# Two attention and dense layers on one core: unread matmuls by the share of the array in use, and a finer table for the banks that VectorE exponentiates

## The chip, the cores and the metric

The kernel runs on one core of a Trainium2 chip. A core has TensorE (PE, matmuls, with PEld for its weight loads), VectorE (DVE), ScalarE (ACT), GpSimd (POOL) and SyncE (SP, which issues the DMAs). The metric is the device time in microseconds of one execution; the time of a version is the median of several executions. The profile shows one execution, with every instruction's start and duration and the clock that was granted to TensorE.

## The reference

The input x has 2048 rows of 448 numbers. Four steps follow one another, each added to x: attention, dense, attention, dense, with the same weights both times.

```python
def _A_ref(x, wqkv, wo):              # H = 16 heads of Dh = 28
    qkv = (x @ wqkv) ...              # q, k, v
    scores = einsum("bhqd,bhkd->bhqk", q, k) * Dh ** -0.5
    p = softmax(scores, axis=-1)
    o = einsum("bhqk,bhkd->bhqd", p, v)
    return o @ wo                     # heads side by side
def _B_ref(x, w1, b1, w2, b2):        # 448 -> 1792 -> 448
    h = x @ w1 + b1
    r = where(h > 0, h, 0)
    return (r * r) @ w2 + b2
x = x + _A_ref(_layernorm(x), A_wqkv, A_wo)
x = x + _B_ref(_layernorm(x), B_w1, B_b1, B_w2, B_b2)
...                                   # both once more
```

The scores are 2 x 16 x 2048 x 2048 numbers, and each of them goes through an exponential.

## The kernel before, in words

**Units and groups.** Scores are made transposed, keys on partitions. A unit is 128 partitions by 512 scores of one head (two key blocks by 256 queries, or four by 128 for the two narrow query blocks at the end), one PSUM bank. There are 2048 units, in passes: a pass is a layer, a query block, four heads that lie on the four row strips of TensorE, and a range of key blocks. `s_stream` takes the units three at a time; such a group has 683 instances. Its score matmuls (L916) use 32 of the 128 rows each, and three strips run side by side. `e_stream` lets ACT take the exponential of a whole group in one instruction (L941). `p_stream` multiplies the probabilities with V (L1080), 128 rows by 32 columns, four heads side by side, and evicts the sums.

**Banks for VectorE.** ACT need not do all. In a group, the function `apart` may give the third bank to VectorE, which computes an exponential in three operations (`a_unit`, `a_rest`): L995 shifts and clamps, L1008 squares the fraction, L1016 adds and writes the bits of a bf16 number. `apart` says no when, among other things, VectorE's backlog (its clock ahead of now, plus what is left of earlier exponentials) exceeds `PACE` at the present place: `PACE` is a table that is spread evenly over the 2048 units. Then ACT takes the third bank as well. The buffers in which VectorE works and the places for its result are limited too (`sets_of`, `pd_free`).

**Everything else** runs in the gaps: layer norm (VectorE, a little POOL), transposes (L551), projections and the dense step in tiles of `mm_tile` (L647) with evictions on VectorE, the spread of the softmax denominators by DMAs, and the sums over w1 (`sums`, L379: 56 matmuls with a single moving column, in seven operations), which are needed for the last block.

**The order of the work** is written by a planner that runs on the host when the kernel is built. Each stream offers its next operation (`Op`) with an engine, a planned duration, what it depends on and which buffer it takes. The planner places the candidate that can start earliest, ties by priority, and holds back TensorE work that would make the next scores late. The order that comes out is fixed in the program; on the chip only semaphores decide when each instruction starts.

**Unread matmuls.** The clock granted to TensorE is not always full (in one stretch of this profile it is 0.50), and the kernel holds matmuls whose result nobody reads, placed by how much TensorE has lately done in the plan. There are two kinds. In `s_stream` a group's score matmuls are repeated, up to `MORE` = 3 times, when `load(HWIN)`, the share of the last 3.4 us in which TensorE was occupied in the plan, is under `HOT` = 0.9 (`HOTE` = 0.8 for the last 100 units), and only as often as they fit before the next TensorE operation and before the buffer's end. In `heat`, the stream of the lowest priority, one or two 448-column matmuls (L1501) are offered after a group when `load(WINDOW)`, over 2.8 us, is under `HEAT` = 0.76. They take one of the two spare PSUM banks for as long as they run.

Of the kernel before, what the change touches and what calls it, by code (L numbers as in the profile page):

```python
# [23 lines left out]


FRAC = 7
EXP_MID = 0.506
EXP_LOW = 128.0 * 128
EXP_SHIFT = 184.0 * 128 - round(EXP_MID * 2.0 ** 16) / 512
# [11 lines left out]
OWN = 2  # L41
HALF = 320
TURNS = 1
ENDU = 100
HOTE = 0.8
WSTOP = ('rs', 0)
XT = 0
VEND = 1
# [3 lines left out]
EARLY = 3  # L52
AHEAD = (range(0, 4), range(0, 4), range(0, 4), range(0, 1))
SLACK = 0.5
WINDOW = 2.8
C_PRIO = 1.6
V_PRIO = 8.5
V_LATE = 5.2
# [13 lines left out]
LEAD = 15  # L72
LAST = 690
BUSY = 0.995
PACE = (3.6, 3.6, 3.6, 1.8, 1.8, 1.8, 1.8, 1.8, 0.3, 0.9, 2.2, 2.2, 2.2, 2.6, 3.0, 3.0, 3.0, 3.6, 6.0, 2.2, 2.2, 2.2, 4.5, 2.2, 3.0, 2.6, 2.2, 2.2, 2.6, 2.6, 1.8, 1.8, 2.2, 2.6, 2.6, 1.8, 1.8, 1.8, 2.2, 2.6, 3.0, 6.0, 2.6, 4.5, 1.4, 1.4, 1.4, 1.4, 1.4, 1.4, 1.4, 1.4, 2.2, 2.2, 2.2, 2.2, 2.2, 2.2, 2.2, 2.2, 2.2, 2.2, 2.2, 2.2)
SPAN = 11
NPT = 11
NOS = 2
AEND = 0
HOT = 0.9  # L80
MORE = 3
HEAT = 0.76
HWIN = 3.4
NEAR_U = 0
LASTP = 3.2
HOLD = 5
# [34 lines left out]


class Op:
    __slots__ = ("eng", "dur", "fn", "deps", "acq", "rel", "mode", "sets", "start", "end", "res", "turn", "ready", "lat", "need", "got", "more", "room")

    def __init__(self, eng, dur, fn, deps=(), acq=None, rel=None, mode="full", sets=(), lat=0.0, need=1):
        self.eng = eng if isinstance(eng, tuple) else (eng,)
        self.dur, self.fn, self.deps, self.mode, self.lat = dur, fn, deps, mode, lat
        self.rel = rel if isinstance(rel, list) else ([] if rel is None else [rel])
        self.acq = acq if isinstance(acq, tuple) or callable(acq) else (() if acq is None else (acq,))  # L130
        self.sets = sets if isinstance(sets, list) else ([sets] if sets else [])
        self.start = self.end = self.res = self.turn = None
        self.need, self.got, self.more = need, [], 0.0


LAT = {"PE": 0.25, "ACT": 0.22, "DVE": 0.10, "POOL": 0.15, "DMA": 2.0, "-": 0.0}
# [2 lines left out]
class Planner:  # L139
# [3 lines left out]
    def __init__(self):  # L143
        self.clock = {"PE": 0.0, "ACT": 0.0, "DVE": 0.0, "POOL": 0.0, "DMA": 0.0, "-": 0.0}
        self.mode = None
        self.tok = {}
        self.streams = []
        self.past = {"PE": [], "DVE": []}
        self.turns = lambda: False
        self.slack = lambda: SLACK  # L150

    def load(self, span, eng="PE"):

        now = self.clock["PE"]
        return sum(min(e, now) - max(s, now - span) for s, e in self.past[eng] if e > now - span and s < now) / span

    def spawn(self, prio, gen):
        self.streams.append([prio, gen, next(gen, None)])
        self.streams.sort(key=lambda s: s[0](0.0) if callable(s[0]) else s[0])

    def earliest(self, o):
        t = 0.0
        for d in o.deps:
            if not isinstance(d, Op):
                d = self.tok.get(d)
            if d is None or d.end is None:
                return None, None
            same = d.eng[0] == o.eng[0] and len(o.eng) == 1
            t = max(t, d.end + d.lat + ((0.03 if same else 0.10) if d.eng[0] == "DVE" else
                                (0.0 if same and d.eng[0] != "DMA" else LAT[d.eng[0]])))  # L170
        acq = o.acq() if callable(o.acq) else o.acq
        if o.acq:
            free = [r.when() for r in acq if r.when() is not None]
            if not free:
                return None, None
            t = max(t, min(free))
        o.ready = t
        best = None
        for e in o.eng:
            s = max(t, self.clock[e])  # L180
            if e == "PE" and self.mode != o.mode:
                s = max(t, self.clock[e] + 0.1)
            if best is None or s < best[0] - 0.05:
                best = (s, e)
        return best

    def run(self):
        while self.streams:
            cands = []
            for st in self.streams:  # L190
                s, e = self.earliest(st[2]) if st[2] is not None else (None, None)
                if s is not None:
                    cands.append((s, st[0](s) if callable(st[0]) else st[0], e, st))
            assert cands, "no stream can go on"
            known = cands

            due = next((c[3][2].ready for c in cands if c[1] == 0), None)
            if due is None:
                due = next((c[0] + c[3][2].dur + LAT["ACT"] for c in cands if c[1] == 1), None)
            if due is not None:  # L200
                ok = [c for c in cands if c[2] != "PE" or c[1] == 0 or c[0] + c[3][2].dur <= due + self.slack()]
                cands = ok or cands
            s, _, e, st = min(cands, key=lambda c: (max(c[3][2].ready, self.clock[c[2]]) if c[2] == "PE" and self.turns() else c[0], c[1]))
            o = st[2]
            o.eng = (e,)
            if o.acq:
                o.res = min((r for r in (o.acq() if callable(o.acq) else o.acq) if r.when() is not None), key=lambda r: r.when())
                o.turn = len(o.res.rel)
                o.res.rel.append(None)
            o.start, o.end = s, s + o.dur  # L210
            if e == "PE":
                o.room = min([c[0] for c in known if c[2] == "PE" and c[3] is not st] or [1e9]) - o.end
            if o.fn:
                o.fn(e)
            o.end += o.more
            self.clock[e] = o.end - (OVER if e == "DVE" and o.dur > 0.1 else 0.0)
            if e == "PE":
                self.mode = o.mode
            if e in self.past:
                self.past[e] = [p for p in self.past[e] if p[1] > s - 40.0] + [(s, max(s, self.clock[e]))]  # L220
            for a in o.rel:
                a.got.append(o.end + o.lat + LAT[e])
                if len(a.got) == a.need:
                    a.res.rel[a.turn] = max(a.got)
            for key in o.sets:
                self.tok[key] = o
            st[2] = next(st[1], None)
            if st[2] is None:
                self.streams.remove(st)
# [3 lines left out]
def kernel(  # L233
# [43 lines left out]
    pl = Planner()  # L277
# [503 lines left out]
    units = []  # L781
# [69 lines left out]
    def s_stream():  # L851
        while at[0] < len(units):
# [5 lines left out]
            def fn(e, gi=gi, us=us, js=js):  # L858
# [41 lines left out]
                    if len(where[pi, kb]) == G:  # L900
                        pl.tok["u", pi, kb] = o

                short = (HOT if len(units) - at[0] > ENDU else HOTE) - pl.load(HWIN)
                again = 0
                if short > 0 and gi > 0:
                    last = ("e" in gbuf[gi - 1] and gbuf[gi - 1]["e"].end) or pl.clock["ACT"] + 1.35
                    again = max(0, min(MORE, int(min(o.room, last - LAT["PE"] - 0.05 - o.end) / 0.22)))
                o.more = 0.22 * again
                for i in list(range(4)) * (again + 1):
                    for k, (pi, kb, r, hh) in enumerate(us):  # L910
                        if i >= r:
                            continue
                        l, qb, g, *_ = passes[pi]
                        t0, nt = blocks[l][qb]
                        rows = slice(DHP * hh, DHP * hh + DHP)
                        nc.tensor.matmul(dst[k][:, i * nt * P:(i + 1) * nt * P],  # L916
                                         lhsT=K_sb[l][rows, g, (kb + i) * P:(kb + i + 1) * P],
                                         rhs=Q_sb[rows, g, t0 * P:(t0 + nt) * P],
                                         start=True, stop=True, tile_position=(DHP * hh, 0))
# [32 lines left out]
    def pd_free(unit):  # L952

        pi, kb, r, hh = unit
        l, qb, *_ = passes[pi]
        if l == 0:
            return (R_pd[0], *(R_pd[1:5] if qb <= 6 else R_pd[3:5]))
        if len(norm_done.get((0, len(blocks[0]) - 1), ())) < G:
            return tuple(R_pd[:1])
        return tuple(R_pd[:1] + R_pd[6:]) if hidden_left[0] else tuple(R_pd[:1] + R_pd[5:])  # L960
# [44 lines left out]
    def a_rest(gi, c, box, unit):  # L1005
# [10 lines left out]
            nc.vector.scalar_tensor_tensor(out=box["two"](pd.bitcast(DT.int16)), in0=box["i"], scalar=EXP_BITS, in1=box["h"],  # L1016
                                           op0=ALU.add, op1=ALU.add)
        own = gbuf[gi]["in"]
        o = Op("DVE", 0.683, close, deps=[h, ("e", gi)] if own else [h], acq=None if own else lambda: pd_free(unit), rel=c, sets=("x", gi))
        gbuf[gi]["x"] = o  # L1020
        yield o
        left[0] -= 0.6
# [6 lines left out]
    def p_stream():  # L1029


        for pi, (l, qb, g, kbs, first, last) in enumerate(passes):
# [19 lines left out]
            while todo:  # L1052
# [16 lines left out]
                def fn(e, now=now, begin=begin, close=close, box=box, pi=pi, l=l, g=g, r=r, n=n):  # L1069
# [4 lines left out]
                    for kb in now:  # L1074
# [13 lines left out]
                       deps=[*by, *{("V", l, kb + i) for kb in now for i in range(r)}],  # L1088
                       acq=None if "o" in box else pools_now(),
                       rel=[gbuf[gi]["e" if w == "x" and gbuf[gi]["in"] else w] for w, gi in by], mode="col")  # L1090
                box.setdefault("o", o)
                yield o
            if last and quick(l, qb, g):
# [392 lines left out]
    def heat():  # L1486


        for gi in itertools.count(HFROM):
            if not s_left:  # L1490
                return
            yield Op("-", 0.0, None, deps=[("s", gi)])
            short = HEAT - pl.load(WINDOW)
            if short <= 0 or not s_left or len(units) - at[0] < HSTOP:
                continue
            k = 1 if short < 0.14 else 2

            def junk(e):
                t = bank(o, "mt")
# [53 lines left out]
```

## Time and profile before

| | |
|---|---|
| median of three executions | 849.33 us (848.26 to 850.94) |
| the profiled execution | 848.74 us, its span 847.0 us |
| mean granted clock | 0.994 |
| ACT busy | 826.4 us, of it 815.7 us in 683 exponentials |
| VectorE busy | 793.7 us |
| exponentials of 3 banks / of 2 banks | 438 / 245 |
| score matmuls / products with V | 5180 / 4352 |
| unread 448-column matmuls (L1501) | 128 |

The span is the time from the first to the last instruction; the rest of the execution's time lies around it. TensorE's busy time counts each matmul with its modelled length, fill and drain included, so it is far from saying that the array streams all that time. In a window's row stand its bounds and length, each engine's busy time with the number of instructions, the granted clock, and the DMA engines' share. In a group's row stand the line of the kernel, the engine, the operation, what it writes and reads, the shape and count, then the busy time and the mean length of one in ns, and the idle time just before them with what ended it. In a waits row stand who waited for whom, the total, how many times, and the longest.

### The profile page before, as it was taken

What the parts mean: (1) busy time and instruction counts of PE and PEld (TensorE: products, weight loads), DVE (VectorE), ACT (ScalarE), POOL (GpSimd) and SP (SyncE); (2) the same over time, 40 slices, a digit from 0 to 9 for tenths busy, and PEclk for the clock granted to TensorE, in tenths of its full rate; (3) what the DMA queues carried; (4) which work ended last, traced back from release to release, by engine and by line L of the source; (5) the groups of instructions that cost most, each with busy time, mean ns of one, the idle gap of its engine ahead of it and who ended that gap; (6) DMA issues with size and microseconds to landing.
All of it is one profiled execution on the core that took longest, in us unless ns stands there. A gap on an engine that the chain in (4) does not pass through costs nothing.

```text
span 847.0 us, 27977 instructions
## 1 busy us (share of the span) xinstructions
PE 809.2 (96%) x12200; PEld 430.6 (51%) x12200; DVE 793.7 (94%) x1563; ACT 826.4 (98%) x699; POOL 41.7 (5%) x94
## 2 busy tenths in 40 slices
PE   8999999999999999999999999998999999999997
PEld 4455555554545545454445554444554454545565
DVE  7999999999999999999899999989999999999965
ACT  8998999999999999999999999999999999999994
POOL 3100000000000010000000000001000000000000
PEclk9999999999999999999999999989999999999999
DMA  9200000000000000000000000011000000000000
GB/s 250 67 2 3 19 24 16 15 16 15 11 6 15 15 16 15 16 3 14 2 3 2 2 2 2 15 30 28 18 24 25 21 21 21 21 13 15 21 9 19
DMA packets 32363, 17.97 MB, mean 21 GB/s; under 512 B 17833, under 2 KB 31787, under 8 KB 32240
## 3 DMA queue, kind: packets, MB, share of 16 engines
q1 hardware_dynamic: 32240, 16.18, 6.9%
q8 instruction: 95, 1.56, 0.8%
q14 instruction: 28, 0.23, 0.1%
HBM read 13.88 MB, written 2.07 MB: 19 GB/s over the span
## 4 chain that ended last, share of the span: by engine, by line
PE 48%; ACT 27%; DVE 15%; issue 7%; DMA 2%; POOL 1%; ACTq 0%; SPq 0%; DVEq 0%
ACT pt L941 27%; PE mt L647 20%; PE sc L916 16%; PE oT L1080 8%; DVE v_i L995 2%; DVE v_h L1008 2%; PE mt L1501 2%; DVE r L1274 1%; DVE pt L1016 1%; DVE K_sb L1008 1%; DVE K_sb L995 1%; DVE st L501 1%; DVE x_sb L1216 1%; DMA rec<-scr 1%; DVE xn L611 1%
## 5 line engine op out<-in xcount | busy, mean ns | idle before, releaser
L941 ACT ACTIVATE pt<-sc 128x1536 bf16<-128x1536 f32 (+1 forms) x683 | 815.7, 1415 | 6.8 <-PE sc L916 6.2
L916 PE MATMUL sc<-Q_sb,K_sb 32*128 32x256 bf16 (+1 forms) x5180 | 306.8, 267 | 27.6 <-ACT pt L941 21.5
L916 PEld LDWEIGHTS <-K_sb 32*128 32x128 bf16 x5180 | 131.6, 92 | 205.9 <-issue 153.1
L1080 PE MATMUL oT<-pt,V_sb 128*32 128x256 bf16 (+1 forms) x4034 | 154.5, 270 | 0.7 <-DVE pt L1016 0.3
L995 DVE TENSOR_SCALAR v_i<-sc 128x512 f32<-128x512 f32 x175 | 119.1, 682 | 6.9 <-PE sc L916 6.1
L647 PE MATMUL mt<-xnT,w 128*128 128x256 bf16 (+1 forms) x888 | 120.3, 271 | 1.0 <-DVE r L1274 0.5
L1008 DVE SCALAR_TENSOR_TENSOR v_h<-v_i 128x512 f32<-128x512 int16 x175 | 117.5, 679 | 0.5
L1080 PEld LDWEIGHTS <-V_sb 128*32 128x32 bf16 x4352 | 90.9, 96 | 50.0 <-issue 46.9
L647 PEld LDWEIGHTS <-w 128*128 128x128 bf16 x896 | 74.3, 98 | 37.7 <-issue 28.9
L1274 DVE TENSOR_SCALAR r<-mt 128x512 bf16<-128x512 f32 x108 | 73.4, 680 | 4.7 <-PE mt L647 4.4
L647 PE MATMUL mt<-w,V_sb 128*128 128x448 bf16 (+1 forms) x288 | 69.3, 348 | 0.0
L995 DVE TENSOR_SCALAR K_sb<-sc 128x512 f32<-128x512 f32 x69 | 47.1, 683 | 3.1 <-PE sc L916 2.4
L528 POOL TENSOR_TENSOR ve<-mv,eps_t 128x2 f32<-128x2 f32 (+1 forms) x33 | 11.5, 348 | 769.3 <-DVE mv L506 769.3
L1008 DVE SCALAR_TENSOR_TENSOR K_sb<-K_sb 128x512 f32<-128x512 int16 x69 | 46.8, 678 | 0.3
L1216 DVE TENSOR_TENSOR x_sb<-x_sb,mt 128x448 bf16<-128x448 bf16 x62 | 37.6, 611 | 7.3 <-PE mt L647 6.8
L1501 PE MATMUL mt<-xn,ident 128*128 128x448 bf16 x128 | 44.1, 357 | 0.3
L1016 DVE SCALAR_TENSOR_TENSOR pt<-v_i,v_h 128x512 int16<-128x512 f32 x64 | 43.0, 672 | 0.3
L1016 DVE SCALAR_TENSOR_TENSOR V_sb<-v_i,v_h 128x512 int16<-128x512 f32 x63 | 42.5, 678 | 0.2
L501 DVE BATCH_NORM_STATS2 st<-x_sb 128x6 f32<-128x448 bf16 x63 | 38.5, 614 | 0.8 <-DMA x_sb<-in_A_x_dram 0.7
L647 PEld LDWEIGHTS <-V_sb 128*128 128x128 bf16 x302 | 24.2, 98 | 25.0 <-issue 11.0
L647 PE MATMUL mt<-wo,oTn 128*128 128x448 bf16 x124 | 31.2, 355 | 0.4 <-DVE r L1274 0.3
L647 PEld LDWEIGHTS <-wk 128*128 128x128 bf16 x256 | 22.2, 97 | 11.4 <-issue 8.3
(133 smaller groups left out, 704.1 us busy)
## 6 DMA issues: line engine op xcount, KB each, us to landing
rec<-scr SPq DMA_DIRECT2D x54, 128.0 KB
x_sb<-in_A_x_dram SPq DMA_DIRECT2D x8, 224.0 KB
out_dram<-x_sb SPq DMA_DIRECT2D x15, 112.0 KB
w<-in_B_w_dram SPq DMA_DIRECT2D x1, 1568.0 KB
w<-in_B_w_dram SPq DMA_DIRECT2D x1, 1344.0 KB
dn<-oT_sb SPq DMA_DIRECT2D x54, 4.0 KB
V_sb<-in_A_wqkv_dram SPq DMA_DIRECT2D x4, 168.0 KB
scr<-dn SPq DMA_DIRECT2D x27, 8.0 KB
```

Source lines behind the costliest of these rows:

```text
L501: nc.vector.bn_stats(out=box["st"][:, :], in_=x_sb[:, t0 + j, :] if src is None else src())
L528: nc.gpsimd.tensor_tensor(out=ve[:, a:b], in0=mv[0][:, a:b, 1], in1=eps_t[:, a:b], op=ALU.add)
L647: nc.tensor.matmul(box["t"][:, c0:c0 + n], lhsT=lhsT() if callable(lhsT) else lhsT, rhs=rhs, start=a, stop=b)
L916: nc.tensor.matmul(dst[k][:, i * nt * P:(i + 1) * nt * P], lhsT=K_sb[l][rows, g, (kb + i) * P:(kb + i + 1) * P], rhs=Q_sb[rows, g, t0 * P: ...
L941: t = nc.scalar.activation(out=pt[:, 0:n], in_=gbuf[gi]["sc"][:, 0:n], func=AF.Exp, scale=float(np.log(2.0)) * 2.0 ** -FRAC)
L995: t = nc.vector.tensor_scalar(out=box["i"], in0=two(src), scalar1=EXP_SHIFT, scalar2=EXP_LOW, op0=ALU.add, op1=ALU.max)
L1008: nc.vector.scalar_tensor_tensor(out=box["h"], in0=box["f"], scalar=EXP_BEND, in1=box["f"], op0=ALU.mult, op1=ALU.mult)
L1016: nc.vector.scalar_tensor_tensor(out=box["two"](pd.bitcast(DT.int16)), in0=box["i"], scalar=EXP_BITS, in1=box["h"], op0=ALU.add, op1=ALU.add)
L1080: nc.tensor.matmul(box["t"][DHP * hh:DHP * hh + DHP, 0:n], lhsT=V_sb[l][:, kb + i, 4 * g + hh, :], rhs=p[:, c0:c0 + n], start=begin and kb ...
L1216: nc.vector.tensor_tensor(out=x_sb[:, tb, lo:hi], in0=x_sb[:, tb, lo:hi], in1=t[:, 0:hi - lo], op=ALU.add)
L1274: nc.vector.tensor_scalar(out=r[:, 0:w], in0=t[:, 0:w], scalar1=0.0, scalar2=None, op0=ALU.max)
L1501: nc.tensor.matmul(t[:, 0:D], lhsT=ident[:, :], rhs=xns[0][:, 0:D], start=True, stop=True)
```

## The change

TensorE's planned use is now measured by how much of its array works. The planner keeps a list `used` of the last TensorE operations with a weight: the time that the same work would take if it filled all of the array. `warm` sums these weights over the last `TICK` = 1.8 us. Scores have 0.0533 us per bank (and repeat), products with V 0.2133 us per step, and all other operations `SHARE` = 0.9 of their planned duration. Both kinds of unread matmuls are added when `warm` is under 0.55; `heat` adds two instead of one when the share is short by more than 0.055 (before 0.14). The constants of the old rule go.

The table `PACE` has 128 entries instead of 64. Their mean is 1.96 instead of 2.38; 75 of the 128 stretches have a lower entry than before, 30 a higher one, 23 the same.

The third operation of VectorE's exponential gets a latency of `XL` = 0.1 us in the plan, for what depends on it and for the buffers that it frees. The planner also keeps the time at which an operation's inputs are there (`base`) rather than working it out each time; that is a matter of the host alone. Since the plan is made step by step, each edit can move everything that is placed after it.

```diff
+XL = 0.1
+TICK = 1.8
+WARM = 0.55
+WARM2 = 0.55
+SHARE = 0.9
...
-ENDU = 100
-HOTE = 0.8
...
-WINDOW = 2.8
...
-PACE = (3.6, 3.6, 3.6, 1.8, 1.8, 1.8, 1.8, 1.8, 0.3, 0.9, 2.2, 2.2, 2.2, 2.6, 3.0, 3.0, 3.0, 3.6, 6.0, 2.2, 2.2, 2.2, 4.5, 2.2, 3.0, 2.6, 2.2, 2.2, 2.6, 2.6, 1.8, 1.8, 2.2, 2.6, 2.6, 1.8, 1.8, 1.8, 2.2, 2.6, 3.0, 6.0, 2.6, 4.5, 1.4, 1.4, 1.4, 1.4, 1.4, 1.4, 1.4, 1.4, 2.2, 2.2, 2.2, 2.2, 2.2, 2.2, 2.2, 2.2, 2.2, 2.2, 2.2, 2.2)
+PACE = (2.2, 2.2, 2.2, 2.2, 2.2, 2.2, 1.0, 1.8, 2.2, 1.0, 2.6, 1.4, 2.2, 1.4, 1.4, 2.2, 2.2, 2.6, 3.0, 1.8, 1.0, 2.6, 2.6, 1.4, 2.2, 2.2, 1.4, 1.4, 1.8, 1.8, 2.2, 1.4, 1.8, 1.4, 0.6, 1.4, 1.8, 1.4, 1.4, 2.2, 1.8, 1.8, 1.8, 3.0, 3.0, 2.2, 2.2, 2.2, 2.2, 2.2, 2.2, 2.2, 2.2, 1.8, 1.8, 2.2, 2.2, 2.2, 2.2, 1.4, 1.4, 2.2, 2.2, 3.0, 3.0, 2.2, 1.8, 1.8, 2.2, 2.2, 1.8, 1.0, 1.0, 1.4, 2.6, 1.8, 1.8, 2.2, 2.2, 1.8, 1.8, 1.8, 1.0, 2.2, 1.8, 3.0, 3.0, 1.8, 1.8, 0.6, 1.0, 1.8, 1.4, 1.4, 0.6, 3.0, 2.2, 1.8, 1.4, 1.4, 0.6, 3.0, 3.0, 1.8, 1.8, 1.8, 1.8, 2.6, 1.4, 1.4, 1.4, 2.2, 2.2, 1.8, 2.2, 1.8, 1.4, 1.8, 1.8, 3.6, 3.6, 3.0, 3.0, 1.4, 2.2, 2.2, 2.2, 2.2)
...
-HOT = 0.9
...
-HEAT = 0.76
-HWIN = 3.4
...
+    def warm(self):
+
+        now = self.clock["PE"]
+        return sum(w * (min(e, now) - max(s, now - TICK)) / (e - s) for s, e, w in self.used if e > now - TICK and s < now) / TICK
...
+            if e == "PE" and o.end > s:
+                self.used = [u for u in self.used if u[1] > s - 2 * TICK] + [(s, o.end, SHARE * o.dur if o.w is None else o.w)]
...
-                short = (HOT if len(units) - at[0] > ENDU else HOTE) - pl.load(HWIN)
+                short = WARM2 - pl.warm()
                 again = 0
                 if short > 0 and gi > 0:
                     last = ("e" in gbuf[gi - 1] and gbuf[gi - 1]["e"].end) or pl.clock["ACT"] + 1.35
                     again = max(0, min(MORE, int(min(o.room, last - LAT["PE"] - 0.05 - o.end) / 0.22)))
                 o.more = 0.22 * again
+                o.w = 0.0533 * len(us) * (again + 1)
...
-        o = Op("DVE", 0.683, close, deps=[h, ("e", gi)] if own else [h], acq=None if own else lambda: pd_free(unit), rel=c, sets=("x", gi))
+        o = Op("DVE", 0.683, close, deps=[h, ("e", gi)] if own else [h], acq=None if own else lambda: pd_free(unit), rel=c, sets=("x", gi), lat=XL)
...
+                o.w = 0.2133 * len(now)
...
-            short = HEAT - pl.load(WINDOW)
+            short = WARM - pl.warm()
             if short <= 0 or not s_left or len(units) - at[0] < HSTOP:
                 continue
-            k = 1 if short < 0.14 else 2
+            k = 1 if short < 0.055 else 2
```

More of the change, by code (lines that the diff above doesn't have):

```diff
@@ L123 @@
 class Op:
-    __slots__ = ("eng", "dur", "fn", "deps", "acq", "rel", "mode", "sets", "start", "end", "res", "turn", "ready", "lat", "need", "got", "more", "room")
+    __slots__ = ("eng", "dur", "fn", "deps", "acq", "rel", "mode", "sets", "start", "end", "res", "turn", "ready", "lat", "need", "got", "more", "room", "base", "w")
     def __init__(self, eng, dur, fn, deps=(), acq=None, rel=None, mode="full", sets=(), lat=0.0, need=1):
@@ L132, in __init__ @@
         self.start = self.end = self.res = self.turn = None
-        self.need, self.got, self.more = need, [], 0.0
+        self.need, self.got, self.more, self.base = need, [], 0.0, None
+        self.w = None
 LAT = {"PE": 0.25, "ACT": 0.22, "DVE": 0.10, "POOL": 0.15, "DMA": 2.0, "-": 0.0}
@@ L148, in __init__ @@
         self.past = {"PE": [], "DVE": []}
+        self.used = []
         self.turns = lambda: False
@@ L161, in earliest @@
     def earliest(self, o):
[L162 to L170, printed above, removed]
+        t = o.base
+        if t is None:
+            t = 0.0
+            for d in o.deps:
+                if not isinstance(d, Op):
+                    d = self.tok.get(d)
+                if d is None or d.end is None:
+                    return None, None
+                same = d.eng[0] == o.eng[0] and len(o.eng) == 1
+                t = max(t, d.end + d.lat + ((0.03 if same else 0.10) if d.eng[0] == "DVE" else
+                                    (0.0 if same and d.eng[0] != "DMA" else LAT[d.eng[0]])))
+            o.base = t
         acq = o.acq() if callable(o.acq) else o.acq
```

## The prediction

> **What bounds the kernel now.** I read the page's busy line first, then the chain, then the two costliest groups, then windows by stage.
>
> ```profile
> PE 809.2 (96%) x12200; PEld 430.6 (51%) x12200; DVE 793.7 (94%) x1563; ACT 826.4 (98%) x699; POOL 41.7 (5%) x94
> L941 ACT ACTIVATE pt<-sc 128x1536 bf16<-128x1536 f32 (+1 forms) x683 | 815.7, 1415 | 6.8 <-PE sc L916 6.2
> PE 48%; ACT 27%; DVE 15%; issue 7%; DMA 2%; POOL 1%; ACTq 0%; SPq 0%; DVEq 0%
> ```
>
> The 683 exponentials of ScalarE alone fill 815.7 of 847.0 us, with 6.8 us of waiting between them. The chain names PE for 48%, which is misleading here: between scores and exponential the chain hops back and forth, and only a wait that ends last costs time. So the windows, split at the opening, the one stretch with a lower clock, and the tail (columns: us, then busy us and count of PE, PEld, DVE, ACT, POOL, then the granted clock):
>
> ```profile
> 0.00:40.00 40.00, 35.54 (x409) 19.50 (x410) 35.11 (x97) 36.53 (x33) 10.44 (x27) 1.00 0.60 168
> 40.00:540.00 500.00, 481.60 (x7074) 251.84 (x7073) 479.91 (x911) 496.35 (x420) 20.75 (x50) 1.00 0.04 10
> 540.00:560.00 20.00, 19.34 (x283) 10.52 (x284) 16.68 (x33) 18.16 (x16) 0.00 (x0) 0.74 0.12 30
> 560.00:800.00 240.00, 231.38 (x3593) 120.79 (x3594) 233.08 (x449) 239.73 (x204) 9.19 (x14) 1.00 0.07 21
> 800.00:847.00 47.00, 41.36 (x856) 27.94 (x850) 28.93 (x78) 35.60 (x31) 1.30 (x3) 1.00 0.06 15
> ```
>
> From 40 to 800 us ACT is idle for 3.65 + 1.84 + 0.27 = 5.8 us of 760. It is simply full. The time can fall there in two ways: fewer banks of scores on ACT, or those 5.8 us. Head and tail hold 3.5 and 11.4 us more, and nothing in the change addresses the tail.
>
> What a bank is worth, from the shapes kept apart, and what it costs on VectorE:
>
> ```profile
> L941 ACT ACTIVATE pt<-sc 128x1536 bf16<-128x1536 f32 x438 | 628.4, 1566 | 4.0 <-PE sc L916 3.6
> L941 ACT ACTIVATE pt<-sc 128x1024 bf16<-128x1024 f32 x245 | 263.6, 1143 | 2.8 <-PE sc L916 2.6
> L995 DVE TENSOR_SCALAR v_i<-sc 128x512 f32<-128x512 f32 x175 | 119.1, 682 | 6.9 <-PE sc L916 6.1
> L1008 DVE SCALAR_TENSOR_TENSOR v_h<-v_i 128x512 f32<-128x512 int16 x175 | 117.5, 679 | 0.5
> L1016 DVE SCALAR_TENSOR_TENSOR V_sb<-v_i,v_h 128x512 int16<-128x512 f32 x63 | 42.5, 678 | 0.2
> ```
>
> Every group takes three banks, on ACT or two there and one on DVE, so the number of groups stays 683 and each bank moved saves ACT 1566 - 1143 = 423 ns and costs DVE 682 + 679 + 678 = 2.04 us. VectorE's idle time is the currency: 20.1 us in 40:540 and 6.9 us in 560:800, 27.0 together, at most 13 banks or 5.6 us. With ACT's 5.8 us that gives a floor for the middle of about 849.3 - 11.4 = 838.
>
> **What VectorE waits for**, 40 to 800 us:
>
> ```profile
> DVE v_i L995 <- PE sc L916: 6.1, 8, 1.5
> DVE K_sb L670 <- PE mt L647: 3.2, 4, 1.2
> DVE Q_sb L666 <- PE mt L647: 2.7, 3, 1.2
> DVE K_sb L995 <- PE sc L916: 2.4, 5, 0.8
> DVE r L1274 <- PE mt L647: 1.8, 4, 0.9
> DVE xnT L563 <- PE tp L551: 1.6, 3, 1.1
> DVE oT_sb L1108 <- PE oT L1080: 1.3, 1, 1.3
> DVE x_sb L1216 <- PE mt L647: 1.0, 2, 0.5
> ```
>
> These are 20.1 us. The stretch with the low clock (waits of 541:562) holds
>
> ```profile
> DVE v_i L995 <- PE sc L916: 1.5, 2, 0.8
> DVE oT_sb L1108 <- PE oT L1080: 1.3, 1, 1.3
> ```
>
> of them, which leaves some 17 us in which VectorE waits for TensorE at full clock.
>
> **Part 1, the unread matmuls.** How many there are now:
>
> ```profile
> L916 PEld LDWEIGHTS <-K_sb 32*128 32x128 bf16 x5180 | 131.6, 92 | 205.9 <-issue 153.1
> L1080 PEld LDWEIGHTS <-V_sb 128*32 128x32 bf16 x4352 | 90.9, 96 | 50.0 <-issue 46.9
> L647 PE MATMUL mt<-xnT,w 128*128 128x256 bf16 x840 | 117.0, 274 | 1.0 <-DVE r L1274 0.5
> L647 PE MATMUL mt<-w,V_sb 128*128 128x448 bf16 x274 | 68.3, 355 | 0.0
> L1501 PE MATMUL mt<-xn,ident 128*128 128x448 bf16 x128 | 44.1, 357 | 0.3
> ```
>
> Each probability tile that L1080 multiplies was made by one score matmul, so 5180 - 4352 = 828 score matmuls are repeats. A column costs (355 - 274) / 192 = 0.42 ns. A set of six repeats (three row strips at once, twice 256 columns) thus takes about 0.22 us, 138 sets 30 us; the 128 of L1501 take 448 x 0.42 = 0.19 us each, 24 us. So unread work occupies an estimated 54 us of TensorE, 6% of the span.
>
> The old rule repeats scores while TensorE was occupied less than 0.90 of 3.4 us, a mark that the plan seldom reaches, so gaps are filled almost wherever a set fits. The new rule counts a set of three banks as 0.16 per 0.22 us, products with V as 0.43 per 0.48, the rest as 0.9, and stops at 0.55. Divided by a mean weight near 0.8 that is an occupation of about 0.69. The 0.76 mark for L1501 comes down less than the 0.90 mark for repeats, but over 1.8 us instead of 2.8 the share swings more, and a shortage over 0.055 now brings two at once. I take it that about half goes, 27 us, with bounds from none to all 54. ACT gains nothing from this directly (it waits 6.8 us in all). VectorE's inputs come earlier: I take half of the 17 us, 8.5 us or four banks, and a fifth from the table below: 5 x 0.423 = 2.1 us. Bounds: no bank, or 17 / 2.04 = 8 banks, 3.5 us; against it a pair of L1501 ahead of a score set, 0.38 us late, hurts only where ACT waits.
>
> **The clock** is what the unread matmuls are for, and the trace has one event. Windows just before and in it, and all of L379 in the first of them:
>
> ```profile
> 544.50:547.90 3.40, 3.40 (x59) 2.31 (x53) 3.34 (x8) 3.40 (x4) 0.00 (x0) 1.00 0.06 8
> 547.90:558.10 10.20, 10.20 (x139) 5.42 (x138) 7.96 (x17) 8.66 (x8) 0.00 (x0) 0.50 0.16 45
> ```
> ```profile
> 544.50:547.90 3.40, 2.33 (x32) 1.86 (x32) 1.00 0.06 8
> ```
> ```profile
> L379 PE MATMUL mt<-onec,w 128*128 128x1 bf16 (+1 forms) x56 | 4.2, 172 | 0.0
> ```
>
> TensorE was "busy" 3.40 of 3.40 us, and then had half its clock for 10.2 us. Of its 59 matmuls 32 were L379's, one column each: busy, but hardly anything streamed. So occupation is indeed the wrong measure. But the new count gives these operations (0.48 us each in the plan, no weight of their own) 0.9 of their length as well, and their order behind everything but L1501 is unchanged: I expect this event again, at the same price. That price: ACT loses 20.00 - 18.16 = 1.8 us, and VectorE 3.3 us, 1.6 banks or 0.7 us: 2.5 us. Bounds: gone, -2.5; one more, +2.5. I take 0. [...]
>
> **Part 2, the table.** The mean bound on VectorE's backlog falls from 2.38 to 1.96 us, and 128 entries stand for 64; an entry lets a bank go to VectorE only while the backlog is below it. Does a low entry starve VectorE? Stretches whose entries are 0.3 and 0.9, then 1.4, then 2.2:
>
> ```profile
> 119.10:145.00 25.90, 24.46 (x385) 13.83 (x377) 24.63 (x49) 25.87 (x22) 2.73 (x4) 1.00 0.06 15
> 577.60:666.30 88.70, 85.56 (x1210) 43.52 (x1211) 86.41 (x169) 88.70 (x76) 3.50 (x6) 1.00 0.08 23
> 679.10:792.00 112.90, 108.57 (x1722) 58.14 (x1715) 109.12 (x209) 112.90 (x98) 4.02 (x6) 1.00 0.06 18
> ```
>
> VectorE is idle 4.9%, 2.6% and 3.3%: between 1.4 and 2.2 there is nothing, below 1.0 some 2%. Eleven new entries are 1.0 or less, about 73 us, so 1.5 us of VectorE, less than one bank; a backlog kept lower elsewhere lets evictions come sooner. I take one bank gained (in the five above), bounds: four lost (1% of 760 us), or the remaining idle time won.
>
> The opening's entries fall from 3.6 to 2.2 and the plan there is drawn anew. ACT waits there:
>
> ```profile
> ACT pt L941 <- PE sc L916: 2.9, 2, 2.2
> PE sc L916 <- DVE K_sb L670: 0.3, 1, 0.3
> ```
>
> These are the waits of 60:100: the scores come late because a K block is cast late. I take half of it, 1.4 us, with bounds of 2.9 gained or another 2.2 lost.
>
> **Small edits.** 0.1 us more after the third VectorE operation orders the products with V a little later; the wait it guards against is 0.3 us in all (the last entry of this row), so 0, covered by other work of TensorE; without that cover, 0.3. Keeping `base` changes no instruction.
>
> ```profile
> L1080 PE MATMUL oT<-pt,V_sb 128*32 128x256 bf16 (+1 forms) x4034 | 154.5, 270 | 0.7 <-DVE pt L1016 0.3
> ```
>
> No DMA, SP or POOL work is added or moved by itself.
>
> **Sum.** -2.1 - 1.4 = -3.5 us. The profiled execution took 848.74 us (span 847.0 and 1.7 around it), which gives 845.2; it lies 0.6 under the median of 849.33, and the same edit on that is **845.8**.
>
> **The rivals.**
> A. No change (0.25): VectorE's waits come from the order of the work (transposes, projection, cast), not from unread work in the way; the 27 us stay, the table gains and loses a bank: 848 to 851. For it: L1501's matmuls run where nothing else is ready, and hardly anything of VectorE waits for them by name:
>
> ```profile
> DVE xn L611 <- PE mt L1501: 0.6, 1, 0.6
> ```
>
> B. The clock falls more often (0.12): less unread work lets single 3.4 us windows drop. At 2.5 us an event, the forecast's 3.5 us are gone at 1.4 events, and three more give 845.8 + 7.5 = 853. Against it: only a window nearly without streaming lost the clock. [...]
> C. The new plan fits worse (0.11): six banks fewer on VectorE and one more wait like the 2.2 us: 849.3 + 2.5 + 2.2 = 854.
> D. Faster (0.52): as summed; with the clock event gone as well, 843.3.
>
> Measurement tells about 0.3%, 2.5 us, from no change: under 846.8 is faster, over 851.9 slower. The likeliest case alone lies in 842 to 847; with A to C the range is 839.5 to 853: its low end takes eight banks, all 2.9 us and the lost event (849.3 - 3.4 - 2.9 - 2.5 = 840.5) and a bank or two from the table.
>
> **What would show it.** Right: L1501 well below 128, L916 below 5180, exponentials of 1024 columns at 250 rather than 245, VectorE's idle time in 40:800 near 20 us, one clock event at L379. Wrong: two or more events at other places, more than 5180 score matmuls, fewer than 240 exponentials of 1024, or ACT's wait for scores above 10 us.

## The result: 0.6% faster, and the profile after

The changed kernel takes 844.27 us (843.94 to 844.65) against 848.92 us of the kernel before on the same chip: ratio of the means 0.9941, 95% interval 0.9923 to 0.9960. The profiled execution took 844.03 us, its span 842.3 us. Some lines of its page, and ACT's shapes kept apart (line numbers are 11 to 13 higher than before):

```profile
PE 786.6 (93%) x11474; PEld 410.7 (49%) x11474; DVE 790.3 (94%) x1561; ACT 824.7 (98%) x698; POOL 43.4 (5%) x94
L953 ACT ACTIVATE pt<-sc 128x1536 bf16<-128x1536 f32 (+1 forms) x683 | 814.6, 1454 | 3.0 <-PE sc L928 2.8
L928 PE MATMUL sc<-Q_sb,K_sb 32*128 32x256 bf16 (+1 forms) x4442 | 279.0, 266 | 44.2 <-ACT pt L953 37.9
L1514 PE MATMUL mt<-xn,ident 128*128 128x448 bf16 x140 | 41.1, 361 | 1.3 <-DVE xnT L574 0.4
```
```profile
L953 ACT ACTIVATE pt<-sc 128x1536 bf16<-128x1536 f32 x439 | 635.8, 1606 | 2.5 <-PE sc L928 2.3
L953 ACT ACTIVATE pt<-sc 128x1024 bf16<-128x1024 f32 x244 | 270.0, 1180 | 0.5 <-PE sc L928 0.5
```

Score matmuls fell from 5180 to 4442, so 90 repeats are left of 828; L1501, now L1514, went from 128 to 140. TensorE instead waits for ACT (37.9 us ahead of scores, 21.5 before). But VectorE has 244 banks, one fewer than before. So the gain is not in banks moved to VectorE. Where it is, the first and last start of the exponentials show (the numbers behind the durations), before, then after:

```profile
L941 ACT ACTIVATE pt<-sc x683: 1018/1485/1752, 10.7 to 831.3; 128x1536 bf16<-128x1536 f32 x107, 128x1024 bf16<-128x1024 f32 x64
```
```profile
L953 ACT ACTIVATE pt<-sc x683: 1017/1531/1802, 10.8 to 826.5; 128x1536 bf16<-128x1536 f32 x111, 128x1024 bf16<-128x1024 f32 x60
```

The last one starts 4.8 us earlier; the head is 0.1 us longer and the tail behind the last exponential is 14.4 us in both. ACT's busy time by stretch, before:

```profile
60.00:100.00 40.00, 37.12 (x32) 1.00 0.04 9
100.00:500.00 400.00, 399.23 (x336) 1.00 0.04 11
500.00:600.00 100.00, 97.89 (x84) 0.95 0.07 19
```

and after:

```profile
60.00:100.00 40.00, 40.00 (x35) 1.00 0.04 9
100.00:500.00 400.00, 400.00 (x337) 1.00 0.04 11
500.00:600.00 100.00, 98.13 (x85) 0.95 0.08 19
```

The idle time of 2.9 us in the opening and 0.8 us in 100 to 500 is gone, that of 2.1 us between 500 and 600 is 1.9. Idle time misses a part, since neighbouring exponentials overlap: their ends, when nothing is late, lie 1.34 us apart (three banks) or 0.92 us (two). The lateness of an end is what it lies beyond that distance. Summed over all ends, lateness falls from 9.2 to 4.0 us: 3.1 to 0.0 in 60 to 100, 1.9 to 0.3 in 100 to 500, 0.6 to 0.2 in 600 to 800, 3.0 to 2.7 in 500 to 600, while the first 60 us have 0.6 and then 0.85. These are 5.2 us less; the bank that came back to ACT takes 0.4 of them, and 4.8 are left.

### The profile page after: what moved, and what is told of

Read it like the earlier page. It is cut to its first block, busy times and chain, and to the rows that moved or that the text cites. A ratio compares the mean times of both kernels' runs of the same rounds, so it can differ in the third digit from the quotient of the medians.

```text
span 842.3 us, 26504 instructions
## 1 busy us (share of the span) xinstructions
PE 786.6 (93%) x11474; PEld 410.7 (49%) x11474; DVE 790.3 (94%) x1561; ACT 824.7 (98%) x698; POOL 43.4 (5%) x94
## 3 DMA queue, kind: packets, MB, share of 16 engines
q8 instruction: 89, 1.46, 0.7%
## 4 chain that ended last, share of the span: by engine, by line
ACT 45%; PE 26%; DVE 16%; issue 11%; DMA 1%; POOL 1%; ACTq 0%; SPq 0%; DVEq 0%
ACT pt L953 45%; PE mt L658 10%; PE sc L928 9%; PE oT L1092 4%; DVE v_i L1007 2%; DVE v_h L1020 2%; DVE r L1287 1%; DVE pt L1028 1%; DVE st L512 1%; DVE K_sb L1020 1%; PE mt L1514 1%; DVE K_sb L1007 1%; PE sc L658 1%; DVE V_sb L1028 1%; DMA rec<-scr 1%
## 5 line engine op out<-in xcount | busy, mean ns | idle before, releaser
L928 PE MATMUL sc<-Q_sb,K_sb 32*128 32x256 bf16 (+1 forms) x4442 | 279.0, 266 | 44.2 <-ACT pt L953 37.9
L928 PEld LDWEIGHTS <-K_sb 32*128 32x128 bf16 x4442 | 109.0, 92 | 224.5 <-issue 172.2
L658 PE MATMUL mt<-xnT,w 128*128 128x256 bf16 (+1 forms) x896 | 116.8, 271 | 0.9 <-DVE r L1287 0.5
L658 PE MATMUL mt<-w,V_sb 128*128 128x448 bf16 (+1 forms) x274 | 67.5, 348 | 0.0
L1028 DVE SCALAR_TENSOR_TENSOR pt<-v_i,v_h 128x512 int16<-128x512 f32 x70 | 47.2, 679 | 0.1
L1514 PE MATMUL mt<-xn,ident 128*128 128x448 bf16 x140 | 41.1, 361 | 1.3 <-DVE xnT L574 0.4
L1028 DVE SCALAR_TENSOR_TENSOR V_sb<-v_i,v_h 128x512 int16<-128x512 f32 x58 | 39.5, 683 | 0.2
L1294 DVE TENSOR_TENSOR V_sb<-r 128x512 bf16<-128x512 bf16 x68 | 28.3, 416 | 0.4
```

Source lines behind the costliest of these rows:

```text
L658: nc.tensor.matmul(box["t"][:, c0:c0 + n], lhsT=lhsT() if callable(lhsT) else lhsT, rhs=rhs, start=a, stop=b)
L928: nc.tensor.matmul(dst[k][:, i * nt * P:(i + 1) * nt * P], lhsT=K_sb[l][rows, g, (kb + i) * P:(kb + i + 1) * P], rhs=Q_sb[rows, g, t0 * P: ...
L1294: nc.vector.tensor_tensor(out=h[:, 0:w // n, :], in0=r, in1=r, op=ALU.mult)
L1514: nc.tensor.matmul(t[:, 0:D], lhsT=ident[:, :], rhs=xns[0][:, 0:D], start=True, stop=True)
```

## The experiments

The lateness just described and the clock are used throughout. Times are medians; a ratio is that of the means, against the kernel before on the same chip. The runs stand on several chips, on which the kernel before takes 848.4 to 849.1 us, so a difference of under a microsecond between two runs says little.

**The two halves, each by itself.** The new rule with the old table, and the old rule with the new table.

```diff
-PACE = (2.2, 2.2, 2.2, 2.2, 2.2, 2.2, 1.0, 1.8, ...   # 128 entries, after
+PACE = (3.6, 3.6, 3.6, 1.8, 1.8, 1.8, 1.8, 1.8, ...   # 64 entries, as before
```


> The changed kernel with the 64-entry table of before: the rule for unread matmuls and the 0.1 us latency alone. Theory R (the rule: the repeats that stood in TensorE's queue made some scores late, and ScalarE's gaps closed when they went): 844 to 846 us, waits of ScalarE for scores near 3 us as in the changed kernel. Theory T (the table: the opening and a few places are laid out better by the new entries): 848 to 850 us, with the two gaps of 2.2 and 0.6 us between 60 and 100 us back.

Measured: 851.51 us, ratio 1.0032 (1.0019 to 1.0044). So neither R nor T. The rule does take away the lateness of 100 to 500 us (1.9 to 0.2), as R has it, but the opening loses as much (3.1 to 4.7), and most of the ten executions have more time at half clock than the kernel before (below). ACT's row of that run in the opening, and the row that begins with the one instruction that waited:

```profile
60.00:100.00 40.00, 35.41 (x31) 1.00 0.02 4
```
```profile
82.71 5.97 ACT L953 ACTIVATE pt<-sc 128x1024 bf16<-128x1024 f32 x5 [4.58 <-PE sc L928]
```

```diff
-PACE = (3.6, 3.6, 3.6, 1.8, 1.8, 1.8, 1.8, 1.8, ...   # 64 entries, before
+PACE = (2.2, 2.2, 2.2, 2.2, 2.2, 2.2, 1.0, 1.8, ...   # 128 entries, as after
```


> The kernel before with the 128-entry table alone, rule and latency as before. Theory R: 848 to 850 us, some 800 repeated score matmuls, ScalarE's waits for scores still 5 us or more. Theory T: 844 to 846 us, and no wait of ScalarE over 0.6 us between 60 and 100 us.

Measured: 867.25 us, ratio 1.0216 (1.0200 to 1.0231), slower than either theory allowed. 249 banks go to VectorE, more than in any other run, and the time is the longest of all. The longer pieces of the chain of waits, and the exponential behind it:

```profile
533.18 0.63 DVE x_sb L1216
533.84 0.64 DVE st L501
535.04 0.70 POOL rstd L529
536.22 1.05 PE tp L551 x8
538.04 3.36 PE mt L647 x12
541.39 0.89 PE sc L916 x11
```
```profile
542.04 4.20 ACT L941 ACTIVATE pt<-sc 128x1024 bf16<-128x1024 f32 x4 [13.48 <-PE sc L916]
```

Layer 1's first scores need the last rows of layer 0: addition, layer norm, transposes, projections. In this plan that whole chain stands alone, and ACT waits 13.5 us; from 535.2 us on TensorE has half its clock in this execution. In the opening this run has 3.9 us of lateness: under the old rule the new entries do not close the gap there. The first of the three operations of VectorE's exponentials, up to 500 us, before, in this run and after:

```profile
0.00:500.00 500.00, 96.96 (x143) 1.00 0.09 23
```
```profile
0.00:500.00 500.00, 99.40 (x146) 1.00 0.08 23
```
```profile
0.00:500.00 500.00, 96.04 (x141) 1.00 0.08 23
```

Five banks more than after are 10 us of VectorE's time by then, which fits a chain that ends late; that they are the cause was not tried.

**The table in parts, under the new rule.** The old and the new entries up to about 105 us, combined with the old and the new ones behind.

```diff
+PACE = new[:16] + old[16:]      # old: each of the 64 entries twice
```


> The changed kernel with the new table's first 16 of 128 entries (up to about 105 us) and the old table behind them. Theory O (under the new rule, the table earns its time in the opening alone): no gap of ScalarE between 60 and 100 us, 844 to 846 us. Theory W (the entries fit the plan everywhere): the opening's gap is gone, but 2 us or more of new gaps stand later, above all between 500 and 600 us where layer 1 begins: 847 us or more.

Measured: 848.64 us, ratio 0.9997 (0.9986 to 1.0008).

```diff
+PACE = old[:16] + new[16:]
```


> The changed kernel with the old table's entries up to about 105 us and the new ones behind them. Theory O: the 4.3 us gap at 84 us is back as with the whole old table, and the time is 848 to 852 us. Theory W: the same gap, and since all that follows is drawn anew, further gaps: more than 852 us.

Measured: 850.60 us, ratio 1.0007 (0.9997 to 1.0017). Together with the run above this makes a square:

| new rule, us | old entries up to 105 us | new entries up to 105 us |
|---|---|---|
| old entries behind | 851.5 | 848.6 |
| new entries behind | 850.6 | 844.3 |

Under the new rule, with its 0.1 us of latency, the opening's gap goes by the opening's entries alone (under the old rule it did not): ACT's rows for 60 to 100 us, with new entries there and old behind, and the other way round:

```profile
60.00:100.00 40.00, 40.00 (x35) 1.00 0.04 9
```
```profile
60.00:100.00 40.00, 35.42 (x31) 1.00 0.02 2
```

That is 4.6 us, but with the old entries behind only 2.9 us arrive at the end by the medians. In the profiled executions two banks fewer go to VectorE (241), and lateness is 2.1 us instead of 0.2 in 100 to 500, 1.9 instead of 0.2 in 600 to 800 and 4.0 instead of 2.3 in between. Part of this is the clock: the execution profiled here had 23.9 us at half clock, that with the whole old table 13.7, and of the 5.9 us of lateness between 500 and 800 us, 4.6 lie in those stretches or within 1.5 us behind them; the 2.1 us ahead of 500 us do not. So W held for the first run (though not "above all" at 500 to 600 us); in the second O's time came true, without W's further gaps. The later entries are worth 0.9 us behind the old opening, which is within the noise, and 4.3 behind the new one.

**How tightly the table fits.** Two edits that are as good as nothing in themselves: no 0.1 us behind VectorE's third operation, and one of 128 entries lower by 0.4.

```diff
-XL = 0.1
+XL = 0.0
```


> The changed kernel without the 0.1 us that the plan adds behind VectorE's third operation. Theory S (that edit is small in itself, as predicted at 0): 843.5 to 845.5 us. Theory F (the table fits only the plan that it stands beside, so any shift of the plan costs): 847 us or more, from new gaps of ScalarE or fewer banks on VectorE, not from TensorE's waits for VectorE's third operation.

Measured: 851.79 us, ratio 1.0033 (1.0023 to 1.0044). 241 banks go to VectorE, and lateness is 2.9 us in 60 to 100 (the opening's gap is back, with the new entries), 5.3 in 500 to 600 and 1.4 in 600 to 800. No wait of TensorE is put down to VectorE's third operation. ACT's waits from 60 to 100 us in this run:

```profile
ACT pt L953 <- PE sc L928: 2.8, 1, 2.8
```

```diff
-PACE = (..., 2.2, 2.6, ...)     # entry 17 of 128
+PACE = (..., 1.8, 2.6, ...)
```


> The changed kernel with one entry of the table (the 17th, for some 6.6 us from about 106 us on) at 1.8 instead of 2.2. Theory S: 843.5 to 845.5 us. Theory F: 847 us or more, though the opening's gap stays away, with the loss in places far behind the entry that was changed.

Measured: 855.68 us, ratio 1.0078 (1.0059 to 1.0098): one entry, which governs 6.6 us at about 106 us, costs 11.4 us. From 60 to 100 us there is no gap; the loss is far away. ACT's rows of that run behind the start of layer 1, and its first and last start:

```profile
582.92 2.96 ACT L953 ACTIVATE pt<-sc 128x1536 bf16<-128x1536 f32 x2 [2.63 <-PE sc L928]
587.34 2.79 ACT L953 ACTIVATE pt<-sc 128x1536 bf16<-128x1536 f32 x2 [1.46 <-PE sc L928]
```
```profile
L953 ACT ACTIVATE pt<-sc x683: 1017/1520/1770, 12.2 to 834.3; 128x1536 bf16<-128x1536 f32 x113, 128x1024 bf16<-128x1024 f32 x58
```

VectorE has 244 banks there, as many as in the changed kernel. The last exponential ends 7.7 us later (1.4 of it ahead of the first one, where that execution had a stretch of 3.4 us at half clock; 1.6 in 100 to 500, 4.0 in 500 to 600, 0.6 in 600 to 800), and the tail behind it is 18.3 us instead of 14.4. Both exponentials that waited there (2.63 and 1.46 us) start in a stretch at half clock (580.9 to 587.7 us), and ahead of the first TensorE itself waited for something that no other run waits for, the DMAs that bring the sums over w1 back:

```profile
PE mt L658 <- DMA w<-sums: 2.4, 2, 1.3
```

In this run these DMAs are issued from 576.4 us on, in the changed kernel from 538.3. So one entry at 106 us has moved the end of the sums by 38 us.

Theory F holds in both runs, with one rival beside it that they do not exclude: the clock. By their granted clock, three of the changed kernel's four executions have 10 us at half clock and one 15. Without the latency it is 14 to 27 us, with the one entry 24 to 34, with the whole old table 14 to 27, with its later entries 14 to 27, with its opening 10 to 20, and under the old rule with the new table 21 to 24. At the 0.2 to 0.34 us for each of these that the last section works out, that is an estimated 1 to 6 us of what they lose: about half of it or more with the old table's later entries (1.7 to 2.9 of 4.3 us), up to about half with the whole old table and with the one entry, the smaller part in the others. Whether a plan that fits worse lowers the clock, or the clock makes the gaps, was not separated.

The third run for it leaves the repeats out of the plan of before and gives it the new table:

```diff
-MORE = 3
+MORE = 0
-PACE = (3.6, 3.6, 3.6, ...      # 64 entries
+PACE = (2.2, 2.2, 2.2, ...      # 128 entries
```


> The kernel before with no repeats of scores in its plan (their number limited to 0) and the new table, with the old rule for the other kind. If the table needs only that the repeats are gone: 844 to 846 us and no gap of 13 us at the start of layer 1. Theory F: 848 us or more, with gaps at places where the changed kernel has none.

Measured: 858.25 us, ratio 1.0115 (1.0096 to 1.0134), with 5.6 us of lateness in 60 to 100 and 7.6 in 500 to 600. So the table does not just need fewer repeats. That it needs this very plan, as F says, fits all three runs, but no run shows it as such.

**What the repeats cost by themselves.** Here the plan of before, and thereby the order of everything else, is kept; the repeated score matmuls are merely not issued.

```diff
-                for i in list(range(4)) * (again + 1):
+                for i in range(4):
```


> The kernel before with its order of work unchanged, but the 828 repeated score matmuls not issued (the 128 of the other kind stay). Theory Q (the repeats stood in TensorE's queue ahead of work that ScalarE waited for): ScalarE's small gaps in 100 to 500 and 600 to 800 us fall from 2.2 us in sum to under 0.5, 846 to 847.5 us, the gap of 2.7 us in 60 to 100 stays. Theory C (the repeats were needed for the clock in this order): more than one stretch at half clock, and 850 us or more. Theory N (neither): 848 to 850 us.

Measured: 848.48 us, ratio 0.9991 (0.9981 to 1.0000), nearest to N. Both mechanisms show. Lateness in 100 to 500 us falls from 1.9 to 0.8 us; that in 60 to 100 stays at 3.1. A second stretch at half clock appears (6.8 us at 521 us beside 10.2 us at 549), and lateness in 500 to 600 rises from 3.0 to 3.7 us. All ten executions have 17 to 25 us at half clock, where most of the kernel before have 10. VectorE's idle time from 40 to 800 us is 30.0 us, about the same as the 30.3 before: the repeats did not make it.

**The clock.** First, no unread matmuls at all behind the opening.

```diff
-WARM = 0.55
-WARM2 = 0.55
+WARM = -1.0
+WARM2 = -1.0
```


> The changed kernel without any unread matmul behind the opening's warm-up (both marks below zero). If the unread matmuls are needed for the clock: several stretches at half clock instead of one, at 1.5 to 2.5 us each, 848 us or more. If nothing but the one-column sums ever lowers the clock: one stretch, 843 to 845 us.

Measured: 862.49 us, ratio 1.0160 (1.0143 to 1.0177). The mean clock of the profiled execution, and its windows just before and in one of eight stretches at half clock:

```profile
core 0: 860.5 us, clock 0.948
```
```profile
390.80:394.20 3.40, 2.05 (x22) 0.83 (x22) 3.40 (x9) 3.40 (x4) 0.00 (x0) 1.00 0.00 0
394.30:401.10 6.80, 6.26 (x44) 2.07 (x47) 5.14 (x12) 4.70 (x5) 0.88 (x2) 0.50 0.00 0
```

The eight stretches add up to 88.7 us. Without unread matmuls the mean clock is 0.945 to 0.950 in the four executions; the changed kernel's profiled execution has 0.994 with 230 of them (90 and 140), the kernel before the same with 956. So in these kernels the clock needs some of them, and far fewer than there were. Since the plan was drawn anew here, part of the 18 us may be misfit as above; of the lateness in 100 to 500 us, 8.9 instead of 0.3, 5.8 us lie in the four stretches there or within 1.5 us behind them.

The one event that stayed, at the sums over w1, was taken up three times. With the seven operations spread out:

```diff
             first = first or last
             yield last
+            yield Op("-", 0.0, None, deps=[("s", len(gbuf) + 3)])
```


> The changed kernel with the seven operations of the sums over w1 placed at least three score groups (some 4 us) apart, nothing left out. If the half clock comes from a 3.4 us window full of one-column matmuls: no such stretch, granted clock 1.00 from start to tail, 842 to 843 us (1.6 us of ScalarE's gaps and 2 us of VectorE's idle time back). If it comes from something else at that place: a stretch of 10.2 us at half clock remains and the time is 844 us.

Measured: 849.57 us, ratio 1.0003 (0.9987 to 1.0020), with three stretches (10.2, 6.8 and 3.4 us) in the profiled execution. Both readings fail: the sums hold one of the two spare banks for 38 us instead of 12, and the plan is another one. Then with the order kept, and unread matmuls among the sums:

```diff
             start=fc == 0 and dc == 0, stop=fc == NFC - 1 and dc == NDC - 1)
+    if fc < NFC - 1:
+        nc.tensor.matmul(box["t"][:, 32:480], lhsT=ident[:, :], rhs=w1[0:P, 0, 0:448], start=False, stop=False)
```


> The changed kernel, its order unchanged, with one unread 448-column matmul behind each four one-column matmuls of the sums over w1 (13 in all, an estimated 2.5 us of TensorE by 0.42 ns a column), in columns of the same bank that nobody reads. If the array's streaming in a 3.4 us window decides the clock: no stretch at half clock, ScalarE's gaps between 500 and 600 us fall from 2.2 to 1 us or less, 842.5 to 843.5 us. If the place loses its clock for another reason: the event stays, and the 2.5 us come on top: 844 to 847 us.

Measured: 845.07 us (844.46 to 846.16), ratio 0.9951 (0.9936 to 0.9965). The clock of the profiled execution, and ACT from 500 to 600 us:

```profile
core 0: 842.7 us, clock 0.999
```
```profile
500.00:600.00 100.00, 98.13 (x85) 1.00 0.07 19
```

The event is gone, as streaming says, and yet ACT is busy 98.13 us there, to the hundredth as with the event. The time went into a new wait: score sets now stand behind the 13 matmuls (the longest, 0.80 us, ends at 530.1 us, behind a run of sums and unread matmuls from 527.7 to 529.6). With 7 of them:

```diff
-    if fc < NFC - 1:
+    if fc % 2 == 0:
```


> As the run that put 13 unread matmuls between the sums over w1, with 7 of them (an estimated 1.3 us of TensorE), one behind each operation's first four one-column matmuls. If streaming decides, the share of the window lies between the one that lost the clock and those that kept it: no stretch at half clock would leave 843 to 844 us, an event 844.5 to 846.

Measured: 846.53 us (842.59 to 848.59), ratio 0.9969 (0.9951 to 0.9988), worse than expected: the profiled execution has a stretch of 13.7 us at half clock, longer than without them. By their granted clock, three of the ten executions have at most 3.4 us at half clock and take 842.6 to 844.4 us; the other seven have 13.5 to 17 us and take 846.2 to 848.6. By its median, no version here beats the changed kernel.

## Why the prediction was right, and where it was not

Time, sign and range were right: forecast -3.5 us, measured -4.65, at 844.27 inside 839.5 to 853. But the larger term of the sum was the wrong one: that the forecast comes out 1.1 us from the measured change is in good part luck.

- **"ACT is simply full"**: right. All the gain is in ACT's waits, 5.2 us of lateness less, out of the 9.2 that were there.
- **"About half goes" of the unread work**: right in size (90 repeats, some 15 sets of 0.22 us, and 140 x 0.19 us make 30 us where there were 54), though I had not expected L1501 to rise.
- **"VectorE's inputs come earlier ... four banks, and a fifth from the table", 2.1 us**: this step failed. VectorE got 244 banks, not 250, and its idle time in 40 to 800 us is 27.9 us after 30.3, not near 20. Its waits for TensorE were not made by the repeats ahead of it: with the order kept and the repeats not issued, its idle time stayed at 30.0 us. In the changed kernel the waits have for the most part merely moved:

```profile
DVE K_sb L1007 <- PE sc L928: 7.0, 5, 2.4
DVE v_i L1007 <- PE sc L928: 5.1, 9, 1.5
```

 Here rival A read the waits better than I did, though its conclusion, no change, was not what followed.
- **"I take half" of the opening's 2.9 us**: too small; all went. Under the new rule it went by the table's first entries, as the square shows, but these alone did not do it: under the old rule 3.9 us of lateness stand there, and without the 0.1 us of latency 2.9. I had put the remaining gaps of ACT at nothing; they gave another 2 us.
- **"I expect this event again, at the same price"**: right on the event (10.2 us at 529 us, behind the sums). The price was about the same: in the stretch itself ACT is idle 1.2 us (1.5 before) and VectorE 2.2 us (2.2). The 2.5 us that I put on it lie within the 2 to 3.5 us estimated in the last section.

```profile
529.20:539.40 10.20, 10.14 (x121) 4.08 (x120) 8.03 (x17) 9.00 (x8) 0.00 (x0) 0.50 0.02 3
```

 So rival B did not come about in the changed kernel, although the run without unread matmuls shows, with a mean clock of 0.948, that leaving them out can cost the clock, and most kernels with part of the change had more half clock than it. That single windows of 3.4 us drop, as B has it, no run shows as such; the stretches themselves were seen, and what they cost.
- **The table "less than one bank", the latency 0**: as averages over a stretch this may hold, but it was the wrong question: the changed kernel without the latency takes 851.79 us, and with one entry lower by 0.4 it takes 855.68. What such an edit does is to redraw all that comes after it. A plan that fits worse, as in rival C, is what all seven kernels with part of the change, or with one small value of it altered, gave: 848.6 to 867.3 us, part of it by the clock, and by waits of ACT rather than by C's six lost banks (they have 241 to 249, before 245). That the changed kernel escaped it was nothing the profile before could show; the 0.11 for C weighed that lightly.

What stays open: how the entries cause each single gap, for instance why the K block of the opening is cast at 78 us in the changed kernel and at 82 in its sister with the old table, was seen but not taken apart, and how much of the loss of the partial kernels is the clock's. Nor was it seen how many of these gaps stand in the plan itself.

## What to carry to other kernels

When one engine is full, list its waits first: 5.2 us less of them made the kernel 4.65 us faster here, while work moved to another engine has first to find that engine idle at the right moment. When an order of work is planned step by step and then corrected by a table, table and rules are one thing: neither half can be judged alone, a 0.4 in one entry cost 11 us here, the clock's part included, and every edit of a duration or a rule asks for a new table. To see what an instruction costs, keep the order and leave out the instruction (0.6 us for 828 repeats, what they do for the clock included); to see what a rule costs, let the plan be drawn anew, and expect much of the second number to be chance. Read the granted clock of every execution beside its time, since a plan drawn anew can change both.

## What the runs showed of the hardware

**What the clock follows.** Just ahead of the half clock TensorE was busy 3.40 of 3.40 us in the kernel before (544.5 to 547.9 us) and in the changed kernel (525.8 to 529.2 us). In the run without unread matmuls it was busy only 2.05 of 3.40 us ahead of the stretch shown above. At full clock there are times like that too, which no half clock followed, one in the kernel before and one in the changed kernel:

```profile
799.80:803.20 3.40, 2.41 (x58) 1.67 (x47) 3.40 (x10) 3.40 (x5) 0.00 (x0) 1.00 0.11 18
```
```profile
503.80:507.20 3.40, 2.28 (x25) 0.92 (x21) 3.40 (x9) 3.40 (x4) 1.74 (x4) 1.00 0.01 2
```

So occupation does not tell them apart in these executions. An estimate from the matmul records of the two profiles does: give each matmul its columns x 0.42 ns, weighted by the share of the array's rows and columns that its record names (a quarter for scores and for products with V), laid before its end. The 3.4 us just ahead of the half clock then have a share of 0.21 in the kernel before and 0.32 in the changed one. Of all times of that length between 40 and 830 us that overlap neither these nor the half clock, the lowest has 0.43 in the kernel before and 0.36 in the changed one. So in these two executions the half clock came behind the time in which, by this estimate, least of the array streamed. The 13 matmuls of 448 columns among the sums fit this: the four executions with them have a mean clock of 0.998 to 1.000. Two events fix no limit, and over how long a time the clock is decided was not shown; the stretches at half clock named here last 3.4, 6.8, 10.2 and 13.7 us. For the mark in the plan's own count, only 0.55 and none at all were run.

Nor does the order alone decide: the profiled execution with 7 unread matmuls had a stretch of 13.7 us, and another of the same kernel had none, by its granted clock of 1.000 (842.59 us). Why they differ was not seen, since only one execution of each kernel has a trace. The times of four kernels (the whole old table, its later entries, the sums spread out, the 7 unread matmuls) spread by 4 to 7 us, and their time at half clock by 14 to 20 us; those of the kernel before lie within 3 us on each chip.

**What a stretch at half clock costs.** In the stretch itself it looks cheap: 10.2 us at half clock left ACT idle for 1.2 to 1.5 us, and 13 matmuls of an estimated 2.5 us that prevent it brought nothing. But the executions of one kernel have the same order of work, and their times rise with the time at half clock, which is twice the span times what the granted clock lacks of 1. Straight lines through the ten executions of each of seven kernels rise by 0.20 to 0.34 us for each microsecond. That makes 10.2 us at half clock an estimated 2 to 3.5 us in all.
